# Four token groups to a slot instead of three in a fused convolution and low-rank mixer

## The chip, the cores and the metric

The kernel runs on one core of a Trainium2 chip. The time is device microseconds of that core for one execution, the median over runs. TensorE is called PE here and its weight loads PEld, VectorE is DVE, ScalarE is ACT, GpSimd is POOL, and SP is the engine that only issues transfers.

## The reference

The input x holds 8 batches of 4224 tokens with 192 channels. The first half is a causal convolution: each of 8 heads (24 channels each) has 7 taps, softmax-normalised, and every token is a weighted sum of itself and the six before it. The second half is a mixer with a low-rank part over tokens and an MLP over channels:

```python
out = np.einsum('hk,bskhg->bshg', w, x_unf)        # convolution: y
xt = x.transpose(0, 2, 1)                          # here x is y
h = xt @ U @ V                                     # U: 4224x32, V: 32x4224
u = x + h.transpose(0, 2, 1)
ch = np.maximum(u @ w_ch1, 0.0) @ w_ch2            # 192 -> 768 -> 192
return (u + ch).astype(np.float32)
```

## The kernel before, in words

A tile is 128 tokens; a batch has 33 tiles and there are 264 in all. A group is 8 tiles, so there are 33 groups (0 to 32), which run across batch ends. The order of all instructions is written out by hand, and every engine works through its own list in that order; semaphores hold an instruction until what it reads is there and what it overwrites is free.

These are the steps:

- `c` is the convolution of one batch, split over several places in a slot. `c4:2:3:A` means batch 4, heads 2 to 4. `conv32` (line 331) makes 8 matmuls a head (line 349) into two PSUM banks and copies each bank to `y_sb` (line 266 on ACT, line 268 on DVE). The letters tell which engine copies, in turn: `A` is ACT for all, `AD` alternates, `AAD` is two on ACT and one on DVE.
- `t` and `s` reduce a batch against U: 33 small matmuls (line 412), a split of the sum into two halves (lines 426 on ACT and 427 on DVE), and two matmuls that add them up (line 438) with a copy on DVE (line 432).
- `w80:88` and `h9` are an h cluster: for tiles 80 to 87 (or group 9) `h_tiles` (matmuls at line 469) makes the low-rank part, two tiles to a PSUM bank, and DVE adds `y_sb` to it (line 492) and writes `u_sb`. All first tiles of the banks come first, then all second ones, so a cluster of 12 tiles asks for its six banks within its first six matmuls. Two tiles of a bank go in one addition, unless a group's half ends between them. When a group is complete, SP issues its transpose into `uT` (line 513).
- `w1` is the first MLP layer of a group: 36 matmuls (line 589) in six steps of two banks, and 12 ReLU copies into `rl_sb`, 7 on ACT (line 603) and 5 on DVE (line 605).
- `w2` is a piece of the second layer: two tiles, 12 matmuls (line 616) into one bank, then DVE adds `u_sb` and writes `out_sb` (line 625), and SP sends it off (line 633). A group has four pieces.

Every matmul result takes a bank from one pool of eight (`psp`), in turn: a matmul that starts a new bank waits until the bank that was taken eight before it has been copied out.

`SLOTS` lists the slots. A slot first does `w1` of all its groups, then the `w2` pieces of its groups, and `at[p]` names the steps that go just ahead of piece p. The slots from number 5 on are built by a loop, with three groups a slot. A slot of numbers 6 to 9 holds one whole convolution (of batch k-2), the `t` and `s` of that batch, and two h clusters, which make the groups of the next slot. `LOADS` says after which step of which group's `w1` the parts of the next batch's x are fetched; POOL issues those and copies x shifted by 32 rows into `xb_sb` (lines 303 to 315).

The pools that matter: `rls` (ReLU outputs, one buffer a group) has 3 buffers, `us` 7, `uts` 5, `outs` 8.

Of the kernel before, what the change touches and what calls it, by code (L numbers as in the profile page):

```python
# [14 lines left out]
def kernel(  # L15
# [12 lines left out]
    B, S, D = x.shape  # L28
# [9 lines left out]
    NG = NTT // GT  # L38
# [9 lines left out]
    ys = ctx.enter_context(tc.tile_pool(name="ys", bufs=3))  # L48
    us = ctx.enter_context(tc.tile_pool(name="us", bufs=7))
    uts = ctx.enter_context(tc.tile_pool(name="uts", bufs=5))  # L50
    rls = ctx.enter_context(tc.tile_pool(name="rls", bufs=3))
    outs = ctx.enter_context(tc.tile_pool(name="outs", bufs=8))
    sml = ctx.enter_context(tc.tile_pool(name="sml", bufs=2))
    psp = ctx.enter_context(tc.tile_pool(name="psp", bufs=8, space=bass.MemoryType.PSUM))
# [588 lines left out]
    def x_load(b, q, after):  # L643
        if q == 0:
# [24 lines left out]
                6: ["t2"],  # L669
                8: ["s2"],  # L670
                9: ["h8"],
                11: ["h9"],
            },
        ),
    ]
    spans = {
        5: [(80, 88), (88, 96), (96, 105)],
        6: [(105, 117), (117, 129)],
        7: [(129, 140), (140, 152)],
        8: [(152, 164), (164, 175)],  # L680
        9: [(175, 187), (187, 198)],
        10: [(198, 210), (210, 222)],
        11: [(222, 233), (233, 245)],
        12: [(245, 253), (253, 264)],
        13: [],
    }
    for k in range(5, 14):
        gs = list(range(3 * k - 9, 3 * k - 6))
        hs = [f"w{t0}:{t1}" for t0, t1 in spans[k]]
        if k == 5:  # L690
            at = {
                2: ["c3:0:3:AAD"],
                3: ["c3:3:3:AAD"],
                4: ["c3:6:2:A", "x4:4"],
                5: [hs[0]],
                6: ["t3"],
                8: ["s3", hs[1]],
                11: [hs[2]],
            }
        elif k < 10:  # L700
            b = k - 2
            at = {
                0: [f"c{b}:0:2:AAD"],
                2: [f"c{b}:2:3:A"],
                4: [f"c{b}:5:3:AD"] + ([f"x{b + 1}:4"] if b + 1 < B else []),
                5: [hs[0]],
                9: [f"t{b}", hs[1]],
                12: [f"s{b}"],
            }
        elif k < 13:  # L710
            at = {0 if k == 12 else 2: [hs[0]], 5 if k == 12 else 7: [hs[1]]}
        else:
            at = {}
        SLOTS.append((gs, gs, at))

    LOADS = {3: [(4, 1), (4, 4), (5, 1), (5, 4)]}
    for b in range(4, B):
        g = 3 * b - 6
        LOADS[b] = [(g, 0), (g, 3), (g + 1, 0), (g + 1, 3)]


# [118 lines left out]
    for gs1, gs2, at in SLOTS:  # L840
# [13 lines left out]
        for p in range(npc + 1):  # L854
            for what in at.get(p, []):
                do(what)
            if p < npc:
                g, k = gs2[p // 4], p % 4
# [35 lines left out]
```

## Time and profile before

| | |
|---|---|
| time, median of 3 runs | 323.36 us (323.28 to 324.11) |
| the profiled execution's own time | 323.12 us |
| its span in the profile | 321.3 us |
| PE busy | 314.9 us, 98% |
| DVE busy | 268.7 us, 84% |
| ACT busy | 169.5 us, 53% |
| POOL busy | 141.6 us, 44% |
| granted PE clock | full in every slice |

Between the span and the profiled execution's time lie 1.8 us that the instruction rows do not cover. Slot 5, the first of the loop, begins at 80.44 us with `w1` of group 6, and the rest of the span to 321.3 us is the loop's slots. Each of slots 5 to 9 takes about 28 us (27.8 us for 108.74 to 136.55), of which 11.76 us is `w1`.

### The profile page before, as it was taken

Reading aid. Unit: us, or ns where it says so; the run is one execution under the profiler, and the core shown is the slowest. Engines: PE = TensorE matmul, PEld = TensorE weight load, DVE = VectorE, ACT = ScalarE, POOL = GpSimd, SP = SyncE. Lnnn points to the kernel's source line nnn. Section 1 sums busy time; section 2 is a strip of 40 time slices with the busy share of each in tenths; the row PEclk is TensorE's granted clock in tenths of the full one; section 3 lists DMA queues with packets and bytes.
Section 4 is the critical chain, followed back from the end, with each engine's and each line's share of the span. In section 5 each row is a group of like instructions: output and inputs, shape, how many; then the busy total and the mean of one; then the engine's idle time right before and its main releaser. Section 6 shows DMA issues by size and latency. Waiting matters only on the chain.

```text
span 321.3 us, 9597 instructions
## 1 busy us (share of the span) xinstructions
PE 314.9 (98%) x4004; PEld 218.7 (68%) x4004; DVE 268.7 (84%) x550; ACT 169.5 (53%) x344; POOL 141.6 (44%) x108
## 2 busy tenths in 40 slices
PE   7999999999999999999999999999999999999996
PEld 3757576478677647946864884686597497487495
DVE  6779989987977986996998699699898888897864
ACT  1766723960874396088249609824904903912910
POOL 8763199529947982993798398000000000000000
PEclk9999999999999999999999999999999999999999
DMA  9999993998997999799799963169077079059035
GB/s 105 191 195 169 196 232 101 196 190 253 210 165 147 263 153 194 189 201 154 191 241 139 191 185 111 52 179 218 2 215 228 3 169 275 2 171 272 2 109 188
DMA packets 122443, 53.39 MB, mean 166 GB/s; under 512 B 87712, under 2 KB 122400, under 8 KB 122400
## 3 DMA queue, kind: packets, MB, share of 16 engines
q1 hardware_dynamic: 84528, 38.08, 46.0%
q0 software_dynamic: 37728, 14.60, 39.6%
q8 instruction: 31, 0.51, 0.7%
q14 instruction: 12, 0.10, 0.1%
q10 hardware_dynamic: 144, 0.10, 0.1%
HBM read 29.22 MB, written 25.95 MB: 172 GB/s over the span
## 4 chain that ended last, share of the span: by engine, by line
PE 91%; ACT 3%; DMA 2%; DVE 2%; POOL 1%; issue 1%; POOLq 0%
PE ps L616 42%; PE ps L589 39%; PE ps L349 3%; PE ps L469 3%; DMA x_sb<-in_x_dram 2%; PE ps L412 2%; ACT rl_sb L603 2%; ACT y_sb L266 1%; PE ps L379 1%; POOL x_sb L79 1%; DVE u_sb L492 1%; DVE rl_sb L605 1%; PE ps L438 0%; PE ps L536 0%; DVE out_sb L625 0%
## 5 line engine op out<-in xcount | busy, mean ns | idle before, releaser
L603 ACT ACTIVATE rl_sb<-ps 128x512 bf16<-128x512 f32 x233 | 124.3, 604 | 89.1 <-PE ps L589 77.6
L616 PE MATMUL ps<-W_sb,rl_sb 128*128 128x192 bf16 x1584 | 139.8, 246 | 0.2
L616 PEld LDWEIGHTS <-rl_sb 128*128 128x128 bf16 x1584 | 128.4, 98 | 12.2 <-issue 11.9
L589 PE MATMUL ps<-uT,W_sb 64*128 64x512 bf16 x1188 | 131.5, 376 | 0.3 <-DVE uT L268 0.2
L605 DVE TENSOR_SCALAR rl_sb<-ps 128x512 bf16<-128x512 f32 x163 | 105.7, 688 | 15.2 <-PE ps L589 14.9
L589 PEld LDWEIGHTS <-W_sb 64*128 64x128 bf16 x1188 | 61.3, 94 | 65.9 <-issue 3.0
L625 DVE TENSOR_TENSOR out_sb<-ps,u_sb 128x384 f32<-128x384 f32 (+1 forms) x133 | 69.5, 550 | 25.9 <-PE ps L616 25.0
L315 POOL COPY xb_sb<-x_sb 32x3072 bf16<-32x3072 bf16 (+1 forms) x24 | 67.7, 2820 | 1.1
L492 DVE TENSOR_TENSOR u_sb<-y_sb,ps 128x192 bf16<-128x192 bf16 (+1 forms) x168 | 65.8, 461 | 0.0
L303 POOL COPY xb_sb<-x_sb 128x3072 bf16<-128x3072 bf16 x12 | 32.9, 2742 | 41.5 <-PE ps L349 33.8
L266 ACT ACTIVATE y_sb<-ps 128x408 bf16<-128x408 f32 (+4 forms) x90 | 38.2, 519 | 11.9 <-PE ps L349 9.8
L79 POOL DMA_DIRECT2D x_sb<-in_x_dram x32 | 27.1, 852 | 12.5 <-PE ps L469 7.7
L268 DVE CAST y_sb<-ps 128x408 bf16<-128x408 f32 (+4 forms) x36 | 19.2, 578 | 1.3 <-PE ps L379 1.2
L426 ACT ACTIVATE tt_hi<-ps 128x192 bf16<-128x192 f32 x8 | 2.6, 330 | 27.4 <-PE ps L412 27.4
L469 PE MATMUL ps<-tt_sb,V_sb 32*128 32x192 bf16 x264 | 12.0, 245 | 0.0
L349 PE MATMUL ps<-x_sb,band 64*32 64x384 bf16 x192 | 11.8, 332 | 0.0
L349 PE MATMUL ps<-xb_sb,band 64*32 64x384 bf16 x192 | 11.8, 331 | 0.0
L469 PEld LDWEIGHTS <-V_sb 32*128 32x128 bf16 x264 | 5.8, 92 | 5.7 <-issue 5.5
L379 PE MATMUL ps<-x_sb,band 64*64 64x240 bf16 (+3 forms) x192 | 8.0, 276 | 0.4 <-DMA x_sb<-in_x_dram 0.3
L379 PEld LDWEIGHTS <-band 64*64 64x64 bf16 x192 | 6.0, 106 | 2.2 <-issue 1.5
L349 PEld LDWEIGHTS <-band 64*32 64x32 bf16 x384 | 4.3, 89 | 4.7 <-issue 2.4
L412 PE MATMUL ps<-y_sb,U_sb 128*32 128x192 bf16 x258 | 7.4, 247 | 0.0
(65 smaller groups left out, 66.5 us busy)
## 6 DMA issues: line engine op xcount, KB each, us to landing
out_dram<-out_sb SPq DMA_DIRECT2D x131, 192.0 KB, 3.0
x_sb<-in_x_dram POOLq DMA_DIRECT2D x14, 384.0 KB, 7.2
x_sb<-in_x_dram POOLq DMA_DIRECT2D x7, 432.0 KB, 7.8
x_sb<-in_x_dram POOLq DMA_DIRECT2D x7, 408.0 KB, 7.2
W_sb<-in_moe_w_ch_dram POOLq DMA_DIRECT2D x3, 288.0 KB, 7.5
x_sb<-in_x_dram POOLq DMA_DIRECT2D x1, 504.0 KB, 7.4
uT<-u_sb SPq DMA_TRANSPOSE x31, 3.8
x_sb<-in_x_dram POOLq DMA_DIRECT2D x1, 480.0 KB, 5.6
```

The source lines that it names most:

```text
L79: return nc.gpsimd.dma_start(out=xt[b][HB * r : HB * r + HB, s0:s1, :], in_=x[b, blk * HB : (blk + s1 - s0) * HB, :].rearrange("(j p) d -> ...
L266: nc.scalar.activation(out=out, in_=in_, func=ACT.Copy)
L303: nc.gpsimd.tensor_copy(out=xbt[b][:, s0:s1, :], in_=xt[b][:, s0 + 1 : s1 + 1, :])
L315: nc.gpsimd.tensor_copy(out=xbt[b][q, s0:s1, :], in_=xt[b][q, s0:s1, :])
L349: nc.tensor.matmul(out=pp[r][QB * cg : QB * cg + QB, 0 : nk[r] * GS], lhsT=w[hr], rhs=t[hr, st : st + 2 * nk[r] - 1 : 2, hs], start=True, ...
L469: last = nc.tensor.matmul(out=banks[pr][:, a * D : (a + 1) * D], lhsT=V_sb[32 * q : 32 * q + 32, (j // 8) * 2 + j % 2, :], rhs=ttb[b][32 * ...
L492: nc.vector.tensor_tensor(out=u_group(g)[:, i : i + n, :, hf, :], in0=yt[b][:, run[0] : run[0] + n, :].rearrange("p n (c k) -> p n c k", c=3),
L589: last = nc.tensor.matmul(out=pps[m][hf][:], lhsT=W1_sb[HB * hf : HB * hf + HB, c, m * P : (m + 1) * P], rhs=uTt[g][HB * hf : HB * hf + HB ...
L603: nc.scalar.activation(out=rl[:, m, hf, :], in_=pp[hf][:], func=ACT.Relu)
L605: nc.vector.tensor_scalar_max(out=rl[:, m, hf, :], in0=pp[hf][:], scalar1=0.0)
L616: last = nc.tensor.matmul(out=cps[:, a * D : (a + 1) * D], lhsT=rlt[g][:, m, hf, (i + a) * P : (i + a + 1) * P], rhs=W2_sb[:, m, :], start ...
L625: nc.vector.tensor_tensor(out=o[:, 0:n, :].rearrange("p n (c k) -> p n c k", c=3), in0=cps[:, 0 : n * D].rearrange("p (n c k) -> p n c k", ...
```

## The change

From group 6 on a slot has four groups instead of three, so that the loop has 7 slots (5 to 11) instead of 9 (5 to 13). The last slot has three groups (30 to 32) in both. A slot of numbers 6 to 9 still holds one batch's convolution, and now three h clusters instead of two; the total of clusters is the same. `rls` gets a fourth buffer. The last cluster of slot 4 makes twelve tiles (72 to 83) instead of the eight of group 9. In slots 6 to 9 the convolution's three parts stand at pieces 0, 3 and 5 instead of 0, 2 and 4, and their copies are assigned otherwise: the first part all on ACT, the second `AAD`, and the third all on ACT, where before they were `AAD`, all ACT and `AD`.

```diff
-    rls = ctx.enter_context(tc.tile_pool(name="rls", bufs=3))
+    rls = ctx.enter_context(tc.tile_pool(name="rls", bufs=4))
...
                 9: ["h8"],
-                11: ["h9"],
+                11: ["w72:84"],
...
-        5: [(80, 88), (88, 96), (96, 105)],
-        6: [(105, 117), (117, 129)],
-        7: [(129, 140), (140, 152)],
-        8: [(152, 164), (164, 175)],
-        9: [(175, 187), (187, 198)],
-        10: [(198, 210), (210, 222)],
-        11: [(222, 233), (233, 245)],
-        12: [(245, 253), (253, 264)],
-        13: [],
+        5: [(84, 94), (94, 103), (103, 113)],
+        6: [(113, 125), (125, 132), (132, 144)],
+        7: [(144, 156), (156, 165), (165, 177)],
+        8: [(177, 189), (189, 198), (198, 210)],
+        9: [(210, 222), (222, 231), (231, 243)],
+        10: [(243, 253), (253, 264)],
+        11: [],
     }
-    for k in range(5, 14):
-        gs = list(range(3 * k - 9, 3 * k - 6))
+    for k in range(5, 12):
+        gs = list(range(4 * k - 14, min(4 * k - 10, NG)))
...
                 5: [hs[0]],
                 6: ["t3"],
-                8: ["s3", hs[1]],
-                11: [hs[2]],
+                8: ["s3"],
+                10: [hs[1]],
+                13: [hs[2]],
             }
         elif k < 10:
             b = k - 2
             at = {
-                0: [f"c{b}:0:2:AAD"],
-                2: [f"c{b}:2:3:A"],
-                4: [f"c{b}:5:3:AD"] + ([f"x{b + 1}:4"] if b + 1 < B else []),
-                5: [hs[0]],
-                9: [f"t{b}", hs[1]],
+                0: [f"c{b}:0:2:A"],
+                3: [f"c{b}:2:3:AAD"],
+                5: [f"c{b}:5:3:A"] + ([f"x{b + 1}:4"] if b + 1 < B else []),
+                6: [hs[0]],
+                9: [hs[1], f"t{b}"],
                 12: [f"s{b}"],
+                14: [hs[2]],
             }
-        elif k < 13:
-            at = {0 if k == 12 else 2: [hs[0]], 5 if k == 12 else 7: [hs[1]]}
+        elif hs:
+            at = {2: [hs[0]], 7: [hs[1]]}
...
-        g = 3 * b - 6
+        g = 4 * b - 10
         LOADS[b] = [(g, 0), (g, 3), (g + 1, 0), (g + 1, 3)]
```

## The prediction

> **What bounds the kernel now.** I read the page first, then the chain of waits in order of time, then the timeline around the slots' edges.
>
> ```profile
> span 321.3 us, 9597 instructions
> ...
> PE 314.9 (98%) x4004; PEld 218.7 (68%) x4004; DVE 268.7 (84%) x550; ACT 169.5 (53%) x344; POOL 141.6 (44%) x108
> ...
> PE 91%; ACT 3%; DMA 2%; DVE 2%; POOL 1%; issue 1%; POOLq 0%
> ```
>
> PE carries the chain, and in the chain in order of time it does so without a break from 67 us to the last output.
>
> ```profile
> 126.50 1.10 PE ps L616 x12
> 127.59 0.43 PE ps L469 x12
> 128.03 4.07 PE ps L616 x48
> ...
> 136.62 11.76 PE ps L589 x108
> ...
> 287.37 7.04 PE ps L616 x84
> ```
>
> Take 48 from 84 matmuls of line 616: 36 cost 7.04 - 4.07 = 2.97 us, so one costs 0.0825 us. Then 48 should take 3.96 and 12 should take 0.99; the rows have 0.11 us more each time. That is what a change to matmuls of another tile shape costs PE. `w1` is 11.76 / 3 = 3.92 us a group, 0.653 us for each of its six steps. These rows repeat in every slot, so there is almost no waiting left to remove: the change can only save changes of shape, and can only lose by new waits for PSUM banks. A wait of the second kind stands ahead of slot 4's `w1`:
>
> ```profile
> 55.41 2.07 DVE L492 TENSOR_TENSOR u_sb<-y_sb,ps 128x192 bf16<-128x192 bf16 x6
> ...
> 55.70 8.24 PE L589 MATMUL ps<-uT,W_sb 64*128 64x512 bf16 x72
> ...
> 57.27 1.17 PEld L589 LDWEIGHTS <-W_sb 64*128 64x128 bf16 x12 [0.37 <-issue]
> ```
>
> 72 matmuls should take 2 x 3.92 = 7.84 us and the row has 8.24 (8.17 to the next matmul). An h cluster just ahead left DVE behind, `w1` took the cluster's banks, and PE stood for 0.3 us. The fifth addition ends at 57.21, PE goes on at 57.27: 0.05 us from the end of a copy to the matmul.
>
> **Shape changes.** From the program's order on PE the shape changes in 132 places before and in 129 after: two slots fewer end and begin a `w1`, but a slot's three clusters, and `s` no longer next to `w1`, give most of it back. 3 x 0.11 = 0.3 us less. All matmuls, copies, transposes and transfers are the same in number. The row of the shape change comes first; the Trainium skill, TensorEngine Tiling (Array Packing), Key Properties, says that changing the tiling mode drains TensorE, which speaks for the change but prices nothing.
>
> **The third convolution part, now all on ACT, one piece ahead of an h cluster.** Slot 6 of before, from the timeline:
>
> ```profile
> 123.48 2.46 ACT L266 ACTIVATE y_sb<-ps 128x384 bf16<-128x384 f32 x6 [1.07 <-PE ps L349]
> ...
> 125.78 0.32 PEld L349 LDWEIGHTS <-band 64*32 64x32 bf16 x24 [0.16 <-issue]
> ...
> 126.21 1.25 ACT L266 ACTIVATE y_sb<-ps 128x384 bf16<-128x384 f32 x3 [0.26 <-PE ps L349]
> 126.36 1.55 DVE L268 CAST y_sb<-ps 128x408 bf16<-128x408 f32 x3
> ...
> 126.43 1.16 PE L616 MATMUL ps<-W_sb,rl_sb 128*128 128x192 bf16 x12
> ...
> 127.52 0.50 PE L469 MATMUL ps<-tt_sb,V_sb 32*128 32x192 bf16 x12
> ...
> 127.97 4.12 PE L616 MATMUL ps<-W_sb,rl_sb 128*128 128x192 bf16 x48
> ```
>
> Count banks back from the cluster: its six take, in turn, the bank of the piece before the convolution and the convolution's banks 1 to 5; the piece behind it takes bank 6. With `AD`, bank 5 is ACT's third copy, done at 126.21 + 1.25 = 127.46, 1.68 us after the convolution's first matmul (125.78), and the cluster starts at 1.74: hidden, just. With `A`, six copies on ACT begin 0.42 us after the first matmul (123.48 against 123.06) and end 2.46 later, at 2.88. A copy is about 0.53 us, so they start (2.46 - 0.53) / 5 = 0.39 apart; the fifth ends at 2.49 and frees its bank at 2.54. The cluster's sixth matmul would start at 1.84 and waits 0.70. The piece behind it would start at 2.19 (127.97); it now comes 0.35 behind the sixth matmul, at 2.89, and its own bank is free at 2.93. The loss is 2.93 - 2.19 = 0.74 us. Behind the waiting matmul stand six matmuls of the cluster and all later pieces; DVE's additions wait for them but have slack, PE has none. Slots 6 to 9: 4 x 0.74 = 3.0 us. Ends: no wait (as under `AD`), or 0.95 a slot if ACT starts 0.2 late; I take the sum, since each row in it is the same work at the same distance. The convolution at pieces 0 and 3 has three pieces (3 us) before its banks are taken, against 2.3 us for four ACT copies: no wait.
>
> A rule that speaks against this edit is in the same page of the Trainium skill, under PSUM Bottleneck: use both ScalarE and VectorE to empty PSUM, since tiling speeds up TensorE alone. Taken as a rule it would count the second part of before (all on ACT, first row above) as a loss too; the trace shows no wait there, for two pieces lie between. By the rule alone all `A` parts would cost; by the rows only the third.
>
> **Slot 4's twelve-tile cluster, one piece ahead of `w1`.**
>
> ```profile
> 79.07 0.34 PE L469 MATMUL ps<-tt_sb,V_sb 32*128 32x192 bf16 x8
> 79.13 1.02 DVE L625 TENSOR_TENSOR out_sb<-ps,u_sb 128x384 f32<-128x384 f32 x2
> ...
> 79.34 1.17 PE L616 MATMUL ps<-W_sb,rl_sb 128*128 128x192 bf16 x12
> 80.06 1.94 DVE L492 TENSOR_TENSOR u_sb<-y_sb,ps 128x384 bf16<-128x384 bf16 x4
> ...
> 80.44 11.90 PE L589 MATMUL ps<-uT,W_sb 64*128 64x512 bf16 x108
> ```
>
> DVE comes to the cluster only at 80.06, and its additions follow each other every (1.94 - 0.55) / 3 = 0.464 us. Six now, then the piece's own: bank k of the cluster is free at 80.06 + 0.464(k-1) + 0.60, the third at 81.59, the fifth at 82.52, the piece's at 83.44. `w1` starts at 80.62 (the cluster is 0.18 longer) and its eight banks are the piece before, the six, and the piece. Its second step wants bank 3 at 81.27 and waits 0.3; the third gets bank 5 at 82.52, and the fourth the piece's bank at 83.44, where it would have been at 80.62 + 3 x 0.653 = 82.58: 0.86 behind. After that DVE's first ReLU copies (every 0.60 us, from the row of seven in 4.27) are just in time. Before, this `w1` takes 11.84 to its next matmul, against 11.76: 0.08 is lost already. Net +0.8 us; ends 0.4 (the row of slot 4 above) and 1.0.
>
> **The last cluster of slots 6 to 9, two pieces ahead of `w1`.** DVE has caught up there, as in the slot where a cluster at 264.28 gets its first addition at 264.86, 0.58 later. Six additions and two pieces: the last piece's bank is free at 0.58 + 7 x 0.464 + 0.60 = 4.43; `w1` starts at 0.45 + 1.99 + 0.10 = 2.54 and asks for it at 2.54 + 3 x 0.653 = 4.50. Slots 7 and 9 begin these tiles at odd numbers, so that three banks need two additions of 0.265 instead of one of 0.464: 0.2 later, 0.13 lost each, 0.26 us together. Ends 0 and 4 x 0.4 (slot 4's row).
>
> **Edits with one answer.** Four groups of `w1` in a row: ACT copies 28 instead of 21, but at 7 x 0.49 = 3.4 us a group (its shortest distance between two, in the rows) against PE's 3.92; DVE 5 x 0.60 = 3.0. No backlog. The fourth `rls` buffer makes `w1` wait for `w2` of four groups before, long done. The clusters of slot 5 and 10 are three or more pieces ahead of a `w1`. SP issues two transposes in a row behind the last cluster (1.4 us each, then 3.8 to land): the later group's lands some 7.5 us after the cluster's start and is read at 2.5 + 11.8 = 14.3; outputs queued behind them have eight buffers. POOL's order is the same, and its x copies get 8 us more a slot.
>
> **The sum.** -0.3 + 3.0 + 0.8 + 0.26 = +3.7 us on 323.12, the profiled execution: 326.8. That execution lies 0.24 under the median of the runs, so I say 327.0.
>
> **The rivals.** *No bank is late* (not slower). The place is the cluster at piece 6: if bank 5 is free by 1.84 us after the convolution's first matmul, its 0.74 is nothing; it decides at 0.70 us earlier than I work out. With slot 4's wait gone too only the shape changes stay: 323.4 - 0.3 = 323.1, no measurable change. For it: ACT is idle 47% of the time. Against: ACT's six copies are one row of 2.46 us, and two such waits stand in slot 4 already. Chance 0.10. *The cluster's wait is gone, the others stay*: 323.4 - 0.3 + 0.8 + 0.3 = 324.2, within 0.3%. 0.05. *The waits pass on to DVE*: the 0.74 delays six additions, and where DVE is then late for the `t` step's second half (`tt_lo`, margin some 0.4 us before `s` at piece 12) and for the last cluster, each of four slots loses up to 1 us more: 331. 0.07. *Four groups spare more than I see*: it would take nine shape changes to pass 0.3%, and the order has three: 0.03, about 322. *The sum above*: 0.75.
>
> **Chances.** Some 0.3%, 1 us, is what a measurement of this kernel tells from no change. Slower 0.82, same 0.15, faster 0.03. Range: the sum with the low ends (1.4 for the cluster's waits at half price, 0.4, 0, less 0.5 if a shape change costs half as much again) is +1.3, 324.7; with the high ends (3.8, 1.0, 1.6, less 0) +6.4, 329.8. I go down to 324.1 to take in the second rival, and leave a little of the top out: 324.1 to 329.3.
>
> **What would show it.** Right: in the profile after, in slots 6 to 9, the L469 row behind the third convolution is 0.7 us longer or broken in two, with the wait ended by ACT's `y_sb`; the first `w1` of slot 5 is 0.8 us longer than 4 x 3.92; the `w1` of slots 7 to 10 stay within 0.2 of 15.7. Wrong: L469 rows of 0.43 us throughout, or a `w1` that starts late for a transpose, or ACT behind in the fourth group.

## The result and the profile after

The changed kernel takes 327.03 us (median of 6 runs, 326.78 to 328.15) against 323.88 us for the kernel before on the same chips. The ratio is 1.0109, with a 95% interval of 1.0094 to 1.0125. The profiled execution took 326.78 us, its span is 325.0 us against 321.3 before: 3.7 us more. The granted PE clock is full in every slice in both. One run of the version with `AD` below took 1797 us and is left out of its ratio.

The page of the changed kernel, with the busy times and the chain by engine:

```profile
span 325.0 us, 9584 instructions
...
PE 317.7 (98%) x4004; PEld 228.6 (70%) x4004; DVE 265.7 (82%) x542; ACT 172.9 (53%) x352; POOL 141.9 (44%) x108
...
PE 87%; ACT 6%; DVE 2%; DMA 2%; issue 1%; POOL 0%; DVEq 0%; POOLq 0%
```

PE is as busy as before (98%), since time in which an earlier matmul is still in flight counts as busy while the next one waits. The chain tells more: ACT's share of it has doubled from 3% to 6%. The chain in order of time shows where, here in slot 6 (start, length, what; the pieces of slots 7 to 9 are the same):

```profile
139.69 0.36 PE ps L349 x5
140.06 2.06 ACT y_sb L266 x5
...
142.16 0.40 PE ps L469 x7
...
142.56 3.13 PE ps L616 x36
```

The chain leaves PE in the middle of the third convolution part, follows five ACT copies, and comes back at the cluster's sixth matmul. The timeline of the same place has the engines side by side:

```profile
140.05 2.47 ACT L266 ACTIVATE y_sb<-ps 128x384 bf16<-128x384 f32 x6 [1.05 <-PE ps L349]
...
141.36 0.26 PE L469 MATMUL ps<-tt_sb,V_sb 32*128 32x192 bf16 x4
...
141.78 0.79 PE L469 MATMUL ps<-tt_sb,V_sb 32*128 32x192 bf16 x8 [0.15 <-ACT y_sb L266]
```

Four matmuls of the cluster start at 141.36, the fifth at 141.78 and the sixth at 142.16. The convolution's first matmul is at 139.62, so the last two are 2.16 and 2.54 us after it. The list of PE's waits now has a line that it did not have before:

```profile
PE ps L469 <- ACT y_sb L266: 0.6, 4, 0.2
```

It lists four waits, one a slot, with 0.6 us in total. That is too little: time in which an earlier matmul is still in flight does not count as idle, and of each slot's two waits only the one ahead of the fifth matmul (0.15 us) is listed. The distance from the cluster's first matmul to the first matmul behind the cluster is the better measure: 1.20 us in each of slots 6 to 9, against 0.45 before. Below, a cluster's row is this distance, and the row at piece 6 is that of the cluster that stands there.

### The profile page after: what moved, and what is told of

Its sections match the earlier page's. It is cut to its first block, busy times and chain, and to the rows that moved or that the text cites. A ratio compares the mean times of both kernels' runs of the same rounds, so it can differ in the third digit from the quotient of the medians.

```text
span 325.0 us, 9584 instructions
## 1 busy us (share of the span) xinstructions
PE 317.7 (98%) x4004; PEld 228.6 (70%) x4004; DVE 265.7 (82%) x542; ACT 172.9 (53%) x352; POOL 141.9 (44%) x108
## 4 chain that ended last, share of the span: by engine, by line
PE 87%; ACT 6%; DVE 2%; DMA 2%; issue 1%; POOL 0%; DVEq 0%; POOLq 0%
PE ps L616 39%; PE ps L589 39%; ACT y_sb L266 4%; PE ps L349 3%; PE ps L469 3%; DMA x_sb<-in_x_dram 2%; PE ps L412 2%; ACT rl_sb L603 2%; DVE u_sb L492 1%; PE ps L379 1%; DVE rl_sb L605 1%; DVE out_sb L625 0%; PE ps L438 0%; PE ps L536 0%; POOL x_sb L79 0%
## 5 line engine op out<-in xcount | busy, mean ns | idle before, releaser
L589 PEld LDWEIGHTS <-W_sb 64*128 64x128 bf16 x1188 | 70.2, 94 | 58.0 <-issue 4.0
L625 DVE TENSOR_TENSOR out_sb<-ps,u_sb 128x384 f32<-128x384 f32 (+1 forms) x133 | 70.6, 551 | 32.6 <-PE ps L616 31.9
L266 ACT ACTIVATE y_sb<-ps 128x384 bf16<-128x384 f32 (+4 forms) x98 | 41.4, 520 | 17.7 <-PE ps L349 15.6
L268 DVE CAST y_sb<-ps 128x408 bf16<-128x408 f32 (+4 forms) x28 | 14.9, 582 | 1.3 <-PE ps L379 1.1
L469 PE MATMUL ps<-tt_sb,V_sb 32*128 32x192 bf16 x264 | 13.7, 246 | 1.2 <-ACT y_sb L266 0.6
```

The source lines that it names most:

```text
L266: nc.scalar.activation(out=out, in_=in_, func=ACT.Copy)
L469: last = nc.tensor.matmul(out=banks[pr][:, a * D : (a + 1) * D], lhsT=V_sb[32 * q : 32 * q + 32, (j // 8) * 2 + j % 2, :], rhs=ttb[b][32 * ...
L589: last = nc.tensor.matmul(out=pps[m][hf][:], lhsT=W1_sb[HB * hf : HB * hf + HB, c, m * P : (m + 1) * P], rhs=uTt[g][HB * hf : HB * hf + HB ...
L625: nc.vector.tensor_tensor(out=o[:, 0:n, :].rearrange("p n (c k) -> p n c k", c=3), in0=cps[:, 0 : n * D].rearrange("p (n c k) -> p n c k", ...
```

## The experiments

The theory was that PE runs without a break, so that the change saves three changes of tile shape and pays for three new waits for PSUM banks. The rivals were that the four-group slots themselves cost something, that any all-ACT part costs the same wherever it stands, or that DVE is the late engine. Times and ratios are against the kernel before, run beside each.

**The letters alone, in the kernel before.**

```diff
-                4: [f"c{b}:5:3:AD"] + ...
+                4: [f"c{b}:5:3:A"] + ...
```

> The kernel before, three groups a slot, with one edit: the third part of the convolution in slots 6 to 9, one piece ahead of an h cluster, is copied by ACT alone. Theory (the letters make the wait, not the four groups): four L469 rows of 1.2 us instead of 0.45, 323.4 + 3.0 = 326.4 us. Rival (the wait needs the longer slot or the other order of the three parts): the rows stay at 0.45 and the time at 323.4. Rival (ACT has a backlog here from the second part, also all on ACT): more than 1.2 us a row, over 327.5.

326.34 us, ratio 1.0099 (1.0086 to 1.0113). All four rows of the cluster behind the third part are 1.20 us. The chain in order of time of this kernel, in slot 6:

```profile
126.19 2.06 ACT y_sb L266 x5
128.25 0.04 issue
128.29 0.40 PE ps L469 x7
```

The same five ACT copies carry the chain, with three groups a slot. The choice of engine one piece ahead of a cluster makes this wait, and the longer slots have no part in it.

**The letters undone, in the changed kernel.**

```diff
-                5: [f"c{b}:5:3:A"] + ...
+                5: [f"c{b}:5:3:AD"] + ...
```

> The changed kernel with one edit: the third part of the convolution in slots 6 to 9 is copied by ACT and DVE in turn (AD) instead of ACT alone. Theory (the h cluster waits for ACT's fifth and sixth copy, 0.75 us in each of four slots): the L469 rows behind the third part go from 1.20 back to 0.45 us and 3.0 us go, 324.0 us in all. Rival (the wait comes from having only one piece between two users of six banks, whoever copies): the rows stay above 1 us and the time stays within 0.5 us of 327.0. Rival (DVE takes the place of ACT as the late one): the rows shrink to half, some 325.5.

The ratio is 1.0074 (1.0059 to 1.0089), against 1.0109 for the changed kernel: the gain is some 1.1 us, not 3. The kernel was run once more for its rows.

> The version with the third part AD once more, for its rows. Theory (DVE, with three copies more, is late for the cluster at piece 9): the L469 rows at piece 6 are 0.45, and those at piece 9 in slots 6 to 9 together 1.2 us longer than the 0.27, 0.35, 0.42 and 0.35 of the changed kernel. Rival (the 1.2 us that are missing of the expected gain lie elsewhere, in the w1 of the longer slots): rows at piece 9 as in the changed kernel.

324.89 us, span 323.1, which is 1.9 less than the 325.0 of the changed kernel. The rows at piece 6 are back at 0.45 us. Those at piece 9 are 0.38, 0.65, 0.84 and 0.65 us instead of 0.27, 0.35, 0.42 and 0.35, which is 1.1 us together: 3.0 us won and 1.1 lost make the 1.9 of the span. Its timeline in slot 8:

```profile
212.85 1.55 DVE L268 CAST y_sb<-ps 128x408 bf16<-128x408 f32 x3
...
214.78 3.06 DVE L492 TENSOR_TENSOR u_sb<-y_sb,ps 128x384 bf16<-128x384 bf16 x9
...
217.52 0.71 PE L469 MATMUL ps<-tt_sb,V_sb 32*128 32x192 bf16 x9
...
217.89 0.11 PEld L469 LDWEIGHTS <-V_sb 32*128 32x128 bf16 x5 [0.28 <-DVE u_sb L492]
```

DVE is busy without a gap from the convolution's three copies through the first cluster's nine additions to 217.8, and the next cluster, which PE reaches at 217.5, has to wait for banks that those additions empty. So all on ACT bought something: it took three copies from DVE, and its own wait held PE back while DVE caught up. No run separates how much each of the two is worth. Undoing the letters uncovers this second wait. The third rival (DVE takes the place of ACT) named the right engine and nearly the right time, but at another cluster.

**How many copies on which engine.** In the changed kernel, two other letters:

```diff
-                5: [f"c{b}:5:3:A"] + ...
+                5: [f"c{b}:5:3:AAD"] + ...
```

```diff
-                5: [f"c{b}:5:3:A"] + ...
+                5: [f"c{b}:5:3:D"] + ...
```

> The changed kernel with one edit: the third part AAD, four copies on ACT and two on DVE. Theory (two waits that trade against each other, ACT's at piece 6 and DVE's at piece 9): bank 5 is ACT's fourth copy, free at 2.17 us, 0.33 late, so the rows at piece 6 are 0.78; those at piece 9 lose 0.2 us in all; 327.0 - 4 x 0.42 + 0.2 = 325.5, no better than AD. Rival (only the wait at piece 6 counts, and AD's loss lies elsewhere): 325.3 + 1.3 = 326.6. Rival (four copies on ACT are early enough): 324.

325.44 us, ratio 1.0052 (1.0034 to 1.0069). The rows at piece 6 are 0.75 us, and only slot 8's at piece 9 is longer (0.47).

> The changed kernel with one edit: the third part in slots 6 to 9 is copied by DVE alone. Theory (six copies on any one engine are too many for one piece's distance): DVE starts after the add of the piece before, 0.6 us after the part's first matmul, with 0.48 us a copy; its sixth bank is free at some 3.6 us, and the cluster's row is 1.8 us instead of 1.2: 4 x 1.4 us over the version with AD, 329.6. Rival (ACT is special, being slower to start): DVE's copies are early enough, rows of 0.45 and 324. Rival (what holds is the number of copies, and DVE's are as ACT's): 327.0.

330.57 us, ratio 1.0222 (1.0203 to 1.0241). The rows at piece 6 are 1.84 us, as expected. The 1 us above the expectation is at piece 9, where DVE's backlog holds the rows to 0.38, 0.65, 0.85 and 0.66.

From `A` by `AAD` to `AD` the wait at piece 6 goes 0.75, 0.30, 0 us a slot, and the one at piece 9 goes the other way: 0.07, 0.13 and 1.2 us in the four slots together, counted over rows of 0.27 and 0.35. By the rows `AAD` and `AD` therefore cost about the same.

**Distance instead of engine.**

```diff
-                6: [hs[0]],
+                7: [hs[0]],
```

> The changed kernel with one edit: the first h cluster of slots 6 to 9 stands at piece 7 instead of 6, so that two pieces and not one lie behind the all-ACT third part. Theory (the fifth bank is free 2.54 us after the part's first matmul, and the cluster now asks for it at 2.8): the wait goes, 3.0 us less, 324.0; DVE has one piece less to catch up before the next cluster at piece 9, and what that costs is under 0.3 us a slot. Rival (an all-ACT part costs what it costs, wherever the cluster is, since ACT is the late engine): 326 to 327. Rival (the next cluster at piece 9 then waits for DVE): the row at piece 9 grows by 0.5 us or more, 325.5 to 326.

326.29 us, ratio 1.0106 (1.0091 to 1.0122). Most of the wait for ACT is indeed gone: the cluster's rows are 0.545 us, 0.1 us over the 0.45 without a wait. This 0.1 is ACT's too. With one piece more in between, the cluster's six banks are those of the convolution, and its sixth matmul takes the bank of ACT's sixth copy. In slot 8:

```profile
213.29 2.47 ACT L266 ACTIVATE y_sb<-ps 128x384 bf16<-128x384 f32 x6 [1.05 <-PE ps L349]
...
215.59 0.61 PE L469 MATMUL ps<-tt_sb,V_sb 32*128 32x192 bf16 x12
```

The sixth copy ends at 213.29 + 2.47 = 215.76, and the cluster's sixth matmul starts at 215.81. The expectation had reckoned with the fifth bank alone. But the rows at piece 9 are 0.54, 0.87, 1.07 and 0.87, longer than in the changed kernel by 1.95 us in all. The chain in order of time of slot 6:

```profile
142.49 0.56 DVE out_sb L625
...
143.42 0.77 DVE u_sb L492 x3
...
144.42 1.09 DVE u_sb L492 x3
```

What carries the chain here is DVE, not ACT. The third rival was right in kind, though the total lies a little above its 325.5 to 326: two pieces between the clusters are too few for the first one's additions. The total therefore says nothing against the theory for piece 6; its row says that two pieces of distance are enough for ACT but for 0.1 us.

**t ahead of the second cluster.** With `AD`, and the order of piece 9 as in the kernel before:

```diff
-                9: [hs[1], f"t{b}"],
+                9: [f"t{b}", hs[1]],
```

> The changed kernel with two edits: the third part AD, and at piece 9 the t step ahead of the h cluster, as in the kernel before, instead of behind it. Theory (the 0.85 us of t on PE are what DVE needs to empty the banks of the cluster at piece 6): the waits at piece 9 go, 1.2 us less than with AD alone, 324.1. Rival (the wait at piece 9 only moves to the pieces behind it, since DVE has the same work): 325.3. Rival (t then waits for ACT or DVE copies of the third part): over 325.5.

324.27 us, ratio 1.002 (1.0004 to 1.0035), as expected. The rows at piece 9 are 0.27, 0.35, 0.46 and 0.35: the 0.85 us of `t`, which needs one bank and not five, give DVE the time that it lacked. The kernel before had this order; the change turned it round.

**Slot 4's cluster.**

```diff
-                11: ["w72:84"],
+                11: ["h9"],
...
-        5: [(84, 94), (94, 103), (103, 113)],
+        5: [(80, 92), (92, 103), (103, 113)],
```

> The changed kernel with one edit: slot 4's last cluster makes eight tiles (group 9) again, and slot 5's clusters begin at tile 80 (12, 11 and 10 tiles). Theory (a cluster of twelve one piece ahead of a w1 is 0.7 us late there): the piece behind the cluster starts 0.28 after it again instead of 0.67, the w1 of group 6 to 9 takes 15.7 instead of 16.2 us, and 0.7 us go, 326.3. Rival (the wait moves to slot 5's larger clusters, which stand closer to its convolution): 327.0.

326.21 us, ratio 1.0097 (1.0079 to 1.0114); the profiled span is 324.3 against 325.0. The first `w1` is 15.72 us instead of 16.22, and the piece starts 0.28 us after the cluster's first matmul instead of 0.67 (0.45 is what a cluster of twelve takes without a wait). Some 0.15 us comes back in slot 5, where the cluster of twelve now takes 0.59. The intervals of this kernel and the changed one overlap, so the rows rather than the totals carry this reading.

**The price of a change of shape.** The kernel before, with the six clusters of slots 10 to 12 split into twelve:

```diff
-        10: [(198, 210), (210, 222)],
+        10: [(198, 204), (204, 210), (210, 216), (216, 222)],
...
```

> The kernel before with one edit: in slots 10 to 12, which have no convolution, each of the six h clusters is split in two at different pieces, so that PE changes its tile shape 12 times more, with the same matmuls and additions. Theory (a change of shape costs PE 0.11 us, and nothing else in these slots waits): 12 x 0.11 = 1.3 us more, 324.7. Rival (the change is hidden by the weight load that runs beside it): 323.4. Rival (smaller clusters free banks and transposes earlier, which is worth something): under 323.2.

324.72 us, ratio 1.0042 (1.003 to 1.0055): 1.36 us (0.97 to 1.78) for 12 changes, 0.11 each (0.08 to 0.15). The chain in order of time of slot 10:

```profile
232.16 2.09 PE ps L616 x24
234.25 0.27 PE ps L469 x6
234.53 2.09 PE ps L616 x24
```

24 matmuls of line 616 are 1.98 us at 0.0825 each, and the rows have 2.09 each time. No wait stands between them.

**All waits away.** Three combinations. The first has the edits for `AD` and for slot 4 from above, and

```diff
-                14: [hs[2]],
+                13: [hs[2]],
```

> The changed kernel with three edits: the third part AD, slot 4's last cluster with eight tiles (group 9) again and slot 5's clusters begun at tile 80 (12, 11 and 10 tiles), and the last cluster of slots 6 to 9 one piece earlier (13 instead of 14). Theory (three new waits of 3.0, 0.7 and 0.2 us are all that the four-group slots cost, and three changes of shape fewer are all that they save): 327.0 - 3.9 = 323.1 us, 0.3 us under the kernel before, hardly to be told from it. Rival (longer slots cost something else as well): above 324. Rival (longer slots save more than the shape changes): under 322.5.

325.0 us, ratio 1.005 (1.0038 to 1.0062), 1.9 us more than expected. Of these, 1.2 us are the wait at piece 9 above, by its rows, and 0.15 are slot 5's cluster of twelve. Some 0.3 us lies outside the span (last section), and the rest is not accounted for.

The second has besides `t` ahead of the cluster, and

```diff
-        5: [(84, 94), (94, 103), (103, 113)],
+        5: [(80, 90), (90, 102), (102, 113)],
...
-            at = {2: [hs[0]], 7: [hs[1]]}
+            at = {0: [hs[0]], 7: [hs[1]]}
```

> The changed kernel with five edits: the third part AD; t ahead of the h cluster at piece 9; the last cluster of slots 6 to 9 at piece 13; slot 4's last cluster with eight tiles again, and slot 5's clusters of 10, 12 and 11 tiles; and the first cluster of slot 10 next to the w1 instead of at piece 2. Theory (with all waits gone, what is left of the four-group slots is four changes of shape fewer than before): 4 x 0.11 = 0.4 us under the kernel before, 322.9 us, a span of 320.9. Rival (there is one more wait behind those): 323.5 to 324.5. Rival (slots of four groups spare more than shape changes): under 322.

324.65 us, ratio 1.0035 (1.002 to 1.0051). Here the cluster at piece 13 comes one piece behind `s`, and the chain shows DVE's copy of `s` as the late one. In slot 8:

```profile
222.73 0.28 DVE tt_sb L432
223.04 0.51 PE ps L469 x12
```

These waits come to 0.9 us in slots 6 to 9 (distances from the last matmul of line 616 to the first of the cluster of 0.25, 0.38, 0.60 and 0.38 us instead of 0.18). Slot 5's larger clusters wait 0.6 us, and the first of slot 10 waits 0.2.

The third has `AD`, `t` ahead of the cluster, the edits for slot 4, and the last cluster at piece 14 again, with

```diff
-                5: [hs[0]],
-                6: ["t3"],
+                6: ["t3", hs[0]],
```

> The changed kernel with four edits: the third part AD; t ahead of the h cluster at piece 9; slot 4's last cluster with eight tiles again, and slot 5's clusters of 12, 11 and 10 tiles; and in slot 5 the first cluster right behind t at piece 6 instead of at piece 5. The last cluster stays at piece 14, two pieces behind s. Theory (each wait that the change brought is gone but 0.1 us in each of slots 7, 8 and 9, and PE changes shape 128 times against 132 before): -0.44 + 0.3 = 0.1 us under the kernel before, no difference that can be measured. Rival (one more wait behind these, as with the last cluster one piece behind s): 0.5 us or more over the kernel before. Rival (four groups a slot spare something else): 0.7 us or more under it.

323.92 us, ratio 1.002 (1.0006 to 1.0034), 0.65 us over the kernel before where no difference was expected. Its profiled span is 321.7 us, against 321.3; 0.3 us of it is a new wait for DVE at slot 5's second and third cluster, and another 0.3 us lies outside the span (last section). No version beat the kernel before. With most waits of this change taken away, four groups a slot come within 0.1 to 0.3% of three: four changes of shape fewer are worth some 0.4 us at 0.11 each, and the waits for DVE that remain and the 0.3 us outside the span take that back.

## Why the prediction was right

The forecast was 327.0 us, and 327.03 was measured, with +3.7 us worked out and +3.7 found in the spans. That the totals agree to 0.03 us is luck: the kernel before took 323.88 us beside the changed one, not the 323.36 that the forecast was built on, and the ratio puts the loss at 3.5 us (3.0 to 4.0). The terms one by one:

- *Third convolution part.* Predicted 0.74 us a slot, with the sixth matmul at 2.54 us after the convolution's first and the next piece at 2.93. Measured: 2.54 and 2.94, a row of 1.20 against 0.45, 4 x 0.75 = 3.0 us. The fifth matmul waits as well, which adds nothing to the sixth's delay. The letters alone, in the kernel before, give the same rows and the same 3 us, so this cause is shown.
- *Slot 4.* Predicted +0.8, measured +0.7, but in part in another place, so that the sum fits better than its parts. I gave the whole wait to `w1`. Its row is 16.22 us, 0.58 over four groups of 3.91, and another 0.22 us stands ahead of it, where the piece behind the cluster waits for the addition of an earlier piece (0.08 of the sum was lost in the kernel before as well):

```profile
77.14 2.00 DVE u_sb L492 x5
79.14 0.48 DVE out_sb L625
...
79.66 1.15 PE ps L616 x12
```

I had read from DVE's late start that it would be late for the cluster's banks, and overlooked that the piece's own bank was held by the same backlog. The eight-tile version takes both away.
- *Last clusters of slots 6 to 9.* Predicted 0.13 us in slots 7 and 9 and none in 6 and 8. The `w1` behind them:

```profile
154.55 15.65 PE ps L589 x144
...
191.41 15.74 PE ps L589 x144
```

These follow slots 6 and 7; slot 8 has 15.65 behind it and slot 9 has 15.74. So 0.10 us is lost behind the clusters that begin at an odd tile, and nothing behind the even ones. They also show that four groups of `w1` in a row bring no ACT backlog, as worked out.
- *Shape changes.* Predicted -0.3 us for three. So small a part of the total cannot be measured; twelve more cost 1.36 us, which gives 0.11 each as the rows had it.
- *The rivals.* No bank late: refuted by the waits. The second rival (324.2) is refuted too, since the wait at piece 6 is there in full. The waits that pass on to DVE, to which I gave a chance of 0.07, hardly occur in the changed kernel (0.07 us in slot 8), but they were nearer than I thought: in the versions with `AD`, and with the cluster at piece 7, they decide the time. The sentence that DVE's additions have slack held by little: with three copies more on DVE, and no wait of PE at piece 6, it fails by 0.1 to 0.5 us a slot at piece 9. I had worked out that DVE would be empty 0.4 us before `s`, and had not asked when it is empty for the cluster at piece 9.
- *The rule of the Trainium skill* that PSUM be emptied by both engines (TensorEngine Tiling (Array Packing), PSUM Bottleneck) agrees with the third part, where `D` alone (ratio 1.0222) and `A` alone (1.0109) are both slower than `AD` (1.0074). The best split depended on what else DVE had to do up to the next cluster, and the first part, all on ACT with three pieces behind it, shows no wait in any run.

## What to carry to other kernels

Where the engine that bounds the kernel runs without a gap, look first at which buffer each of its instructions takes and who empties it, counted back by the size of the pool. Here the price of the rearrangement was the sum of a few waits, each of which could be worked out from the start, the step and the number of copies on the emptying engine. A wait on the bounding engine can be the slack that another engine lives on, so that removing it uncovers the next one: an edit that took away a wait of 3.0 us gave back 1.9 of the span. Longer slots saved nothing here that shows beyond the changes of shape that they avoid; count those in the program's order on the engine before expecting anything of them.

## What was not expected of the hardware

The part of the time that the span does not cover was 1.74 to 1.88 us in the runs of the changed kernel and of the other experiments, but 2.10 to 2.15 us in the five runs of the version with three edits and 2.09 to 2.19 us in the twelve runs with four edits. Both have `AD` and slot 5's clusters of 12, 11 and 10 tiles, which no other version has together. This 0.3 us lies outside the instruction rows and stays unexplained; without it the version with four edits would be within 0.1% of the kernel before.
